# FFT filter and gated FFN in one kernel: batches 1 to 7 transformed inside the FFN of the batch before

## The chip, the cores and the metric

One core of a Trainium2 chip runs the kernel. The metric is device time in microseconds (us). TensorE (PE), VectorE (DVE), ScalarE (ACT) and GpSimd (POOL) compute; SyncE (SP) issues most DMAs; each engine takes its instructions in order.

## What is computed

For eight batches of 3136 positions and 256 channels, a filter is applied in the frequency domain; the result goes through a gated feed-forward network (FFN) with 1024 inner channels.

```python
X = np.fft.rfft(x, axis=1)
Y = X * (filt_r + 1j * filt_i)[None]
x = np.fft.irfft(Y, n=3136, axis=1)

h = np.maximum(x @ w_in, 0.0)
conv_out = sum(conv_w[k] * hp[:, k:k + S, :] for k in range(3))   # hp: h padded by one on both sides
gate = 1.0 / (1.0 + np.exp(-conv_out))
out = (h * gate) @ w_out
```

## The kernel before

**The transform.** 3136 = 112 x 28, so a batch goes through four steps of small f32 matmuls, each in 14 pieces of two column groups. *First* (F, `first`, L317): DFT over 112 rows with the table `s1`, then a copy to SBUF and a store to `a_dram`. *Second* (S, `second`, L324): reads `a_dram` in another order, DFT over 28. *Filter* (`filt`, L334): three DVE multiplications straight from PSUM with the tables `t1` and `t2`, then an addition on POOL. *Third* (T, `third`, L347): inverse over 28 with the table `i1`, a copy and a store to `b_dram`. *Last* (L, `last_stage` and `last_out`, L210 and L219): reads `b_dram`, inverse over 112 with `m2`, and splits the result into a high and a low fp32r part, `y` (ACT writes the high part, DVE subtracts for the low part). Two batches of `y` are held at a time. Going through DRAM turns the data: a batch's S reads need all its F stores, L reads all its T stores.

**The front.** One loop (L366) over 112 pieces of all eight batches, F some 18 pieces ahead of S, filter and T. All tables stay in SBUF; the lower half of the filter tables is copied to the upper partitions by ACT (`copy_filter`). The FFN weights, float64 in DRAM, are converted to fp32 in bits (`to_f32`: seven DVE operations and a POOL addition for each of eight blocks) and split, one step in most iterations. At the end L of batch 0 runs.

**The FFN.** 448 units: a unit is one of 28 stretches of 896 positions (`j`), one of eight groups of 128 inner channels (`f`) and one half of the stretch (`i`). In iteration m each engine has, in the order written out by hand (`manual_schedule`):

- PE: `inner` (six fp32r matmuls into a PSUM bank `ps_h`), an L piece if there is one, `project` of unit m - 6 (4 or 3 tiles of three matmuls into `po`);
- ACT: relu of unit m - 1 and its scaled copy, sigmoid of m - 2, high part of g of m - 3, high part of y of an L piece;
- DVE: two conv steps of unit m - 1, the gate product of m - 2, low part of y, and after the last `f` the copies of `po` (`evacuate`).

The eight PSUM banks are four of `ps_h` (shared by `inner` and L in turn) and four of `po`. L of batch b runs in the FFN of batch b - 1, 14 pieces over its units except those that are 3 to 7 modulo 16:

```python
free = [m for m in range(start, stop) if m % 16 not in AVOID]
```

A copy of `po` comes when m - 6 is the last `f`, so in units 4 and 5 modulo 16. The SP queue is not part of the hand-written order.

Of the kernel before, what the change touches and what calls it, by code (L numbers as in the profile page):

```python
# [9 lines left out]
F32 = mybir.dt.float32  # L10
F32R = mybir.dt.float32r
I32 = mybir.dt.int32
# [7 lines left out]
G = 28  # L20
# [18 lines left out]
def _dft_tables():  # L39
# [68 lines left out]
    i1 = np.concatenate([i1[0], np.zeros((8, G, 112)), i1[1]])  # L108
# [16 lines left out]
def tile_fft_filter_gated_ffn(  # L125
# [5 lines left out]
    nyq: bass.AP,  # L131
# [54 lines left out]
    m2_sb = wc.tile([112, N1], F32, name="m2_sb")  # L186
    cw = wc.tile([128, 3, NF], F32, name="cw")
# [4 lines left out]


    ys, yps = {}, []
    lasts = {}

    def last_load(b, c):
        br = lp.tile([112, 2, D], F32, name="br", bufs=4)
        nc.sync.dma_start(out=br, in_=b_dram[b][c:c + 2].rearrange("n p d -> p n d"))
        lasts[b, c] = br  # L200

    def y_slices(b, sl):
        if sl.start == 0:
            ys[b] = [yps[b % 2].tile([128, KT, S + 2], F32R, name=f"y{h}") for h in range(2)]
            for t in ys[b]:
                nc.gpsimd.memset(t[:, :, 0:1].bitcast(F32), 0.0)
                nc.gpsimd.memset(t[:, :, S + 1:S + 2].bitcast(F32), 0.0)
        return (t[:, :, 1:S + 1].rearrange("p k (a c) -> p k c a", c=N2)[:, :, sl] for t in ys[b])

    def last_stage(b, c, ps):  # L210

        br = lasts[b, c]
        for j in range(2):
            for k in range(KT):
                o = ps[:, (2 * k + j) * N1:(2 * k + j + 1) * N1]
                nc.tensor.matmul(o, lhsT=br[:, j, 128 * k:128 * k + 128], rhs=m2_sb, start=True, stop=True)  # L216
        lasts[b, c] = ps

    def last_out(b, c):  # L219
        yh, yl = y_slices(b, slice(c, c + 2))  # L220
        pv = lasts.pop((b, c))[:, 0:4 * N1].rearrange("p (k c a) -> p k c a", c=2, a=N1)
        hi_act(yh, pv)
        lo_dve(yl, pv, yh)

    forward_pools = ExitStack()
    xp = forward_pools.enter_context(tc.tile_pool(name="xp", bufs=2, side="right"))
    s1_sb = xp.tile([112, N2, 112], F32, name="s1_sb", bufs=1)
    with (
        tc.tile_pool(name="fc", bufs=1) as fc,
        tc.tile_pool(name="fp", bufs=2) as fp,  # L230
# [3 lines left out]
        s2_sb = fc.tile([112, 120], F32, name="s2_sb")  # L234
        s2s_sb = fc.tile([112, 120], F32, name="s2s_sb")
        i1_sb = fc.tile([120, G, 112], F32, name="i1_sb")

        turned = [fc.tile([120, 2, D], F32, name=f"v{k}") for k in range(2)]
        for v in turned:
            nc.gpsimd.memset(v[32:64], 0.0)  # L240
        t1_sb = fc.tile([120, G, D], F32, name="t1_sb")
        t2_sb = fc.tile([120, G, D], F32, name="t2_sb")

        rows = {}

        def load_filter(c):
            sl = slice(4 * c, 4 * c + 4)
            for t, src in ((t1_sb, fr), (t2_sb, fi)):
                nc.sync.dma_start(out=t[0:64, sl], in_=src[:, sl])

        def copy_filter(c):
            sl = slice(4 * c, 4 * c + 4)
            nc.scalar.activation(t1_sb[64:120, sl], t1_sb[0:56, sl], AF.Copy)
            nc.scalar.activation(t2_sb[64:120, sl], t2_sb[0:56, sl], AF.Copy, scale=-1.0)
            if c == 6:
                nc.sync.dma_start(out=t1_sb[92:93, G - 1], in_=nyq)

        raws = {}

        def load_weights(k):  # L260
            raws[k] = raw = cv.tile([128, 2, 512], I32, name="raw")
# [3 lines left out]
        def convert_conv():  # L265
            n = 3 * NF
            raw = cv.tile([128, 2, 512], I32, name="raw")
            nc.sync.dma_start(out=raw[:, 0, 0:2 * n], in_=conv_w)
            yield
            em = cv.tile([128, 2, 512], I32, name="em", bufs=1)  # L270
            yield from to_f32(cw.rearrange("p k f -> p (k f)"), raw[:, 0, 0:2 * n], em[:, 0, 0:n], em[:, 1, 0:n])

        def convert_weights():

            for k in range(8):
# [9 lines left out]
                for part, (wh, wl) in enumerate(parts):  # L285
                    lo_pool(wl, ws[:, part], wh)
                    yield
                if k < 6:
                    load_weights(k + 2)

        NP = 14
        parts = {}
        psums = {}

        def pool(kind):
            return xp if kind in ("x", "sa") else fp

        def load(kind, b, p):
            r = pool(kind).tile([112, 2, D], F32, name=kind, bufs=8 if kind == "x" else 5)
            if kind == "x":  # L300
                v = x[b].rearrange("(p n) d -> p n d", n=N2)
            else:
                v = a_dram[b].rearrange("n (r g) d -> (n r) g d", g=G)
            nc.sync.dma_start(out=r, in_=v[:, 2 * p:2 * p + 2])
            rows[kind, b, p] = r

        def store(kind, b, p, ps):
            st = pool(kind).tile([112, 2, D], F32, name=kind, bufs=4)
            nc.scalar.activation(st, ps, AF.Copy)
            sl = slice(2 * p, 2 * p + 2)  # L310
            if kind == "sa":
                v = a_dram[b][sl].rearrange("n p d -> p n d")
            else:
                v = b_dram[b].rearrange("n (r g) d -> (n r) g d", g=G)[:, sl]
            nc.scalar.dma_start(out=v, in_=st)

        def first(b, p):  # L317
            r = rows.pop(("x", b, p))
            ps = fps.tile([112, 2, D], F32, name="ps")
            for j in range(2):  # L320
                nc.tensor.matmul(ps[:, j], lhsT=s1_sb[:, 2 * p + j], rhs=r[:, j], start=True, stop=True)  # L321
            return ps

        def second(b, p):  # L324
            r = rows.pop(("a", b, p))
            pp = fps.tile([120, 2, D], F32, name="pp", bufs=3)
            if p < NP - 1:
                nc.tensor.matmul(pp, lhsT=s2_sb, rhs=r, start=True, stop=True)  # L328
            else:
                for j, m in ((0, s2_sb), (1, s2s_sb)):  # L330
                    nc.tensor.matmul(pp[:, j], lhsT=m, rhs=r[:, j], start=True, stop=True)
            psums[b, p] = pp

        def filt(b, p):  # L334


            pp, v = psums.pop((b, p)), turned[p % 2]
            sl = slice(2 * p, 2 * p + 2)
            u = fp.tile([120, 2, D], F32, name="u")
            nc.vector.tensor_mul(u, pp, t1_sb[:, sl])  # L340
            nc.vector.tensor_mul(v[64:120], pp[0:56], t2_sb[0:56, sl])  # L341
            nc.vector.tensor_mul(v[0:56], pp[64:120], t2_sb[64:120, sl])  # L342
            z = fp.tile([120, 2, D], F32, name="z", bufs=3)
            nc.gpsimd.tensor_tensor(out=z, in0=u, in1=v, op=ALU.add)  # L344
            parts["z", b, p] = z

        def third(b, p):  # L347
            z = parts.pop(("z", b, p))
            ps = fps.tile([112, 2, D], F32, name="ps")
            for j in range(2):  # L350
                nc.tensor.matmul(ps[:, j], lhsT=i1_sb[:, 2 * p + j], rhs=z[:, j], start=True, stop=True)  # L351
            return ps

        def at(i):
            return divmod(i, NP) if 0 <= i < NP * B else None

        SKEW = NP + 4
        nc.sync.dma_start(out=s1_sb[:, 0:4], in_=s1[:, 0:4])
        load("x", 0, 0)
        load("x", 0, 1)  # L360
        for c in range(1, 4):
            nc.sync.dma_start(out=s1_sb[:, 4 * c:4 * c + 4], in_=s1[:, 4 * c:4 * c + 4])
            load("x", 0, 2 * c)
            load("x", 0, 2 * c + 1)
        csteps, wsteps = convert_conv(), convert_weights()
        done = NP * B + 6  # L366
        NI = max(NP * B + SKEW + 5, done + N2 // 2 + 3)
        with tc.manual_schedule(engines=COMPUTE):
            for i in range(NI):
                f, m = i, i - SKEW  # L370
                if i == done:
                    forward_pools.close()
                    yps.append(ctx.enter_context(tc.tile_pool(name="y_even", bufs=1, side="right", reuse_waits="tile")))
                    lp = ctx.enter_context(tc.tile_pool(name="lp", bufs=2, side="right", reuse_waits="tile"))
                if 1 <= i < 4:
                    nc.sync.dma_start(out=s1_sb[:, 4 * i + 12:4 * i + 16], in_=s1[:, 4 * i + 12:4 * i + 16])
                if (bp := at(f + 7)) and i:
                    load("x", *bp)
                if bp := at(m + 3):
                    load("a", *bp)  # L380
                if i == 6:
# [3 lines left out]
                if 12 <= i < 26 and i % 2 == 0:  # L385
                    sl = slice((i - 12) // 2 * 4, (i - 12) // 2 * 4 + 4)
                    load_filter(i // 2 - 6)
                    nc.sync.dma_start(out=i1_sb[:, sl], in_=i1[:, sl])
                if bp := at(m - 2):
                    filt(*bp)  # L390
                pt = third(*bp) if (bp := at(m - 4)) else None
# [174 lines left out]
```

## Time and profile before

| | |
|---|---|
| median of 3 runs | 1575.55 us (1572.48 to 1576.59) |
| profiled execution, its span | 1573.9 us |
| first FFN matmul (L177) in it | 385.1 us |
| moved by DMA | 166.83 MB |
| mean granted TensorE clock | 0.984 |

The span is the time from the first to the last instruction of one profiled execution; the runs' times are of other executions. In the profile's rows "PE" is a matmul and "PEld" a weight load beside it; "x" gives the count; the last columns of a windows row are granted clock, DMA share and GB/s. A row of the timeline is start, duration, engine, line, and in brackets the idle time before and what ended it.

### The profile page before, as it was taken

What the parts mean: (1) busy time and instruction counts of PE and PEld (TensorE: products, weight loads), DVE (VectorE), ACT (ScalarE), POOL (GpSimd) and SP (SyncE); (2) the same over time, 40 slices, a digit from 0 to 9 for tenths busy, and PEclk for the clock granted to TensorE, in tenths of its full rate; (3) what the DMA queues carried; (4) which work ended last, traced back from release to release, by engine and by line L of the source; (5) the groups of instructions that cost most, each with busy time, mean ns of one, the idle gap of its engine ahead of it and who ended that gap; (6) DMA issues with size and microseconds to landing.
All of it is one profiled execution on the core that took longest, in us unless ns stands there. A gap on an engine that the chain in (4) does not pass through costs nothing.

```text
span 1573.9 us, 26330 instructions
## 1 busy us (share of the span) xinstructions
PE 1510.8 (96%) x9424; PEld 1351.0 (86%) x9424; DVE 1280.7 (81%) x1965; ACT 1192.6 (76%) x2162; POOL 698.0 (44%) x624
## 2 busy tenths in 40 slices
PE   5699999998999999999999999999999999999998
PEld 4366666656999999999999999999999999999998
DVE  0487878897888888888888888888888888888887
ACT  3444444445988888888888888888888888888887
POOL 0255555562444444444444444444444444444444
PEclk8699999999999999999999999999999999999999
DMA  9999999984111011111111111111111111100001
GB/s 292 298 345 349 341 309 338 340 251 142 30 48 48 30 48 48 48 48 48 40 33 36 47 48 49 46 48 47 36 42 48 48 37 41 48 24 25 24 24 48
DMA packets 128278, 166.83 MB, mean 106 GB/s; under 512 B 10682, under 2 KB 87571, under 8 KB 128147
## 3 DMA queue, kind: packets, MB, share of 16 engines
q1 hardware_dynamic: 86931, 113.74, 23.1%
q10 hardware_dynamic: 41216, 51.39, 9.9%
q8 instruction: 75, 1.23, 0.3%
q14 instruction: 56, 0.46, 0.1%
HBM read 88.03 MB, written 77.07 MB: 105 GB/s over the span
## 4 chain that ended last, share of the span: by engine, by line
PE 83%; DMA 9%; DVE 4%; ACT 2%; issue 1%; ACTq 0%; POOL 0%; SPq 0%; DVEq 0%; POOLq 0%
PE ps_h L178 12%; PE ps_h L179 12%; PE ps_h L177 11%; PE po L473 11%; PE po L475 11%; PE po L474 11%; PE ps_h L216 5%; PE ps L321 4%; DMA x<-in_x 3%; PE ps L351 3%; PE pp L328 3%; DMA a<-a_dram 2%; DMA a_dram<-sa 2%; DVE y L149 1%; DVE v L341 1%
## 5 line engine op out<-in xcount | busy, mean ns | idle before, releaser
L152 POOL TENSOR_TENSOR g<-t,g 128x448 fp32r<-128x448 f32 x448 | 517.6, 1156 | 667.6 <-ACT g L146 265.8
L473 PE MATMUL po<-wo,g 128*128 128x256 f32 x1568 | 441.5, 282 | 0.0
L475 PE MATMUL po<-wo,g 128*128 128x256 f32 x1568 | 433.8, 277 | 0.0
L474 PE MATMUL po<-wo,g 128*128 128x256 f32 x1568 | 433.4, 276 | 0.0
L447 DVE SCALAR_TENSOR_TENSOR t<-ps_h,cw,t 128x448 f32<-128x448 f32 x448 | 305.5, 682 | 83.9 <-ACT t L442 73.3
L178 PE MATMUL ps_h<-y,wi 128*128 128x450 f32 x896 | 330.8, 369 | 4.2 <-DVE y L149 4.2
L177 PE MATMUL ps_h<-y,wi 128*128 128x450 f32 x896 | 329.2, 367 | 3.4 <-ACT y L146 2.1
L179 PE MATMUL ps_h<-y,wi 128*128 128x450 f32 x896 | 329.2, 367 | 0.0
L448 DVE SCALAR_TENSOR_TENSOR t<-ps_h,cw,t 128x448 f32<-128x448 f32 x448 | 306.4, 684 | 16.0
L442 ACT ACTIVATE t<-ps_h,cw 128x448 f32<-128x448 f32 x448 | 285.2, 637 | 42.1 <-ACT ps_h L440 0.7
L473 PEld LDWEIGHTS po<-wo,g 128*128 128x128 f32 x1568 | 294.7, 188 | 7.0
L474 PEld LDWEIGHTS po<-wo,g 128*128 128x128 f32 x1568 | 294.3, 188 | 5.7
L475 PEld LDWEIGHTS po<-wo,g 128*128 128x128 f32 x1568 | 294.4, 188 | 0.0
L440 ACT ACTIVATE ps_h<-ps_h 128x450 f32<-128x450 f32 x448 | 251.6, 562 | 32.5 <-PE ps_h L179 27.7
L453 DVE TENSOR_TENSOR t<-ps_h,t 128x448 f32<-128x448 f32 x448 | 275.1, 614 | 0.1
L452 ACT ACTIVATE t<-t 128x448 f32<-128x448 f32 x448 | 255.1, 569 | 12.2 <-DVE t L448 11.0
L146 ACT ACTIVATE g<-t 128x448 fp32r<-128x448 f32 x448 | 254.4, 568 | 0.2 <-DVE t L453 0.2
L344 POOL TENSOR_TENSOR z<-u,v 120x512 f32<-120x512 f32 x112 | 157.2, 1404 | 169.5 <-DVE v L342 144.8
L177 PEld LDWEIGHTS ps_h<-y,wi 128*128 128x128 f32 x896 | 170.4, 190 | 12.0 <-ACT y L146 3.3
L179 PEld LDWEIGHTS ps_h<-y,wi 128*128 128x128 f32 x896 | 168.6, 188 | 13.9
L178 PEld LDWEIGHTS ps_h<-y,wi 128*128 128x128 f32 x896 | 168.6, 188 | 13.5 <-DVE y L149 6.6
L149 DVE TENSOR_TENSOR y<-ps_h,y 128x448 fp32r<-128x448 f32 x98 | 103.1, 1052 | 76.7 <-ACT y L146 76.7
(51 smaller groups left out, 1447.5 us busy)
## 6 DMA issues: line engine op xcount, KB each, us to landing
x<-in_x SPq DMA_DIRECT2D x112, 224.0 KB, 4.6
a_dram<-sa ACTq DMA_DIRECT2D x112, 224.0 KB, 4.5
a<-a_dram SPq DMA_DIRECT2D x112, 224.0 KB, 4.7
b_dram<-sb ACTq DMA_DIRECT2D x112, 224.0 KB, 4.1
br<-b_dram SPq DMA_DIRECT2D x112, 224.0 KB, 2.6
out<-ot SPq DMA_DIRECT2D x27, 896.0 KB, 4.1
raw<-in_w_in SPq DMA_DIRECT2D x8, 256.0 KB, 4.6
raw<-in_w_out SPq DMA_DIRECT2D x8, 256.0 KB, 5.3
```

Source lines behind the costliest of these rows:

```text
L152: nc.gpsimd.tensor_tensor(out=dst, in0=src, in1=hi.bitcast(F32), op=ALU.subtract)
L177: nc.tensor.matmul(ps, lhsT=wh, rhs=rh, start=start, stop=False, **kw)
L178: nc.tensor.matmul(ps, lhsT=wh, rhs=rl, start=False, stop=False, **kw)
L179: nc.tensor.matmul(ps, lhsT=wl, rhs=rh, start=False, stop=stop, **kw)
L442: nc.scalar.activation(t, h[:, 1:SUB + 1], AF.Copy, scale=cw[:, 1, f:f + 1])
L447: nc.vector.scalar_tensor_tensor(out=t, in0=h[:, 0:SUB], scalar=cw[:, 0, f:f + 1], in1=t, op0=ALU.mult, op1=ALU.add)
L448: nc.vector.scalar_tensor_tensor(out=t, in0=h[:, 2:SUB + 2], scalar=cw[:, 2, f:f + 1], in1=t, op0=ALU.mult, op1=ALU.add)
L452: nc.scalar.activation(t, t, AF.Sigmoid)
L453: nc.vector.tensor_mul(t, h[:, 1:SUB + 1], t)
L473: nc.tensor.matmul(o, lhsT=gh[:, sl], rhs=wo[0][:, f], start=first, stop=False, skip_group_check=True)
L474: nc.tensor.matmul(o, lhsT=gh[:, sl], rhs=wo[1][:, f], start=False, stop=False, skip_group_check=True)
L475: nc.tensor.matmul(o, lhsT=gl[:, sl], rhs=wo[0][:, f], start=False, stop=last, skip_group_check=True)
```

## The change

The front keeps the weight conversion, all steps of batch 0, and F of batch 1. F of batches 2 to 7, and S, filter and T of batches 1 to 7, become FFN steps, one step a unit (in nine units of batch 1's stretch two). Steps are laid out in `slots`; their loads are issued three or four units ahead (`loads`, `begin`). The tables are no longer held: each step loads its slice of `s1`, or of both filter halves (now 128 partitions, negation in a DVE operation) and `i1`.

```diff
+    def filt(b, p, pp):
+        t1, t2, v = tables.pop(("t1", b, p)), tables.pop(("t2", b, p)), turned[p % 2]
+        u = tp.tile([120, 2, D], F32, name="u", bufs=1)
+        nc.vector.tensor_mul(u, pp, t1[0:120])
+        nc.vector.tensor_mul(v[64:120], pp[0:56], t2[0:56])
+        nc.vector.scalar_tensor_tensor(out=v[0:56], in0=pp[64:120], scalar=-1.0, in1=t2[64:120], op0=ALU.mult, op1=ALU.mult)
...
+    def store(kind, b, p, ps, eng):
+        st = tp.tile([112, 2, D], F32, name="st")
+        nc.scalar.activation(st, ps, AF.Copy)
...
+        eng.dma_start(out=v, in_=st)
...
+    def second_third(b):
+        seq = [("S", b, 0), ("S", b, 1)]
+        for p in range(2, NP):
+            seq += [("T", b, p - 2), ("S", b, p)]
+        return seq + [("T", b, NP - 2), ("T", b, NP - 1)]
+
+    def first_last(b):
+        seq = [("F", b + 1, p) for p in range(4)]
+        for p in range(4, NP):
+            seq += [("L", b, p - 4), ("F", b + 1, p)]
+        return seq + [("L", b, p) for p in range(NP - 4, NP)]
+
+    slots = {k: [op] for k, op in enumerate(second_third(1))}
+    for p in range(4):
+        slots[2 * NP + p] = [("F", 2, p)]
+    for p in range(NP):
+        slots[32 + p * 15 // (NP - 1)] = [("L", 1, p)]
+    for p in range(4, NP):
+        slots.setdefault(28 + p, []).insert(0, ("F", 2, p))
+    for b in range(2, B):
+        seq = second_third(b)
+        if b < B - 1:
+            seq += first_last(b)
+        for k, op in enumerate(seq):
+            slots[56 * b - 64 + k] = [op]
+    for p in range(NP):
+        slots[56 * B - 88 + p * 23 // (NP - 1)] = [("L", B - 1, p)]
...
+    for m, ops in slots.items():
+        for op in ops:
+            loads.setdefault(m - {"F": 4, "S": 3, "T": 3, "L": 3}[op[0]], []).append(op)
```

The front is three loops: F of batch 0 with the conversion (60 of its 80 steps inside, the rest behind); S, filter and T of batch 0 with ten F pieces of batch 1; L of batch 0 with the last four F pieces. In the FFN `inner` has three PSUM banks (h0 to h2; four once no step is left) and all transform steps the fourth, h3. `gate` loses its sigmoid to a function of its own; every second copy of `po` goes to ACT; the output tile `ot` has one buffer; SP joins the hand-written order and issues the stores. The loop is now:

```diff
+            for s in loads.get(m, ()):
+                begin(s)
+            done, works = works, []
+            ops = slots.get(m, [])
             if a := at(m):
-                inner(*a)
-            if m in pieces:
-                last_stage(*pieces[m], ps_h.tile([128, 512], F32, name="ps_h"))
+                n = 4 if m > end else 3
+                inner(*a, f"h{turn % n}")
+                turn = turn % n + 1
+            if ops:
+                works.append(multiply(ops[0]))
             if a := at(m - PLAG):
                 project(*a)
+            lows = []
             if a := at(m - 1):
                 relu(*a)
-                conv(*a)
+            for w in done[:1]:
+                lows.append(on_act(w))
             if a := at(m - 2):
-                gate(*a)
+                sigmoid(*a)
             if a := at(m - 3):
                 split_g(*a)
-            if m in pieces:
-                last_out(*pieces[m])
+            for w in done[1:]:
+                lows.append(on_act(w))
+            filtered = [w for w in done if w[0][0] == "S"]
+            for (kind, b, p), ps in filtered:
+                filt(b, p, ps)
+            if filtered and (a := at(m - 2)):
+                gate(*a)
+            if a := at(m - 1):
+                conv(*a)
+            for lo in lows:
+                if lo:
+                    lo()
+            if not filtered and (a := at(m - 2)):
+                gate(*a)
+            if ops[1:]:
+                works.append(multiply(ops[1]))
             if a := at(m - PLAG):
                 evacuate(*a)
```

`multiply` runs a step's matmuls into h3. `on_act` runs in the next iteration: the copy and store of an F or T step, or the high part of an L step, whose low part is put in `lows`.

More of the change, by code (lines that the diff above doesn't have):

```diff
@@ new lines, in stage1, with stage2 @@
+    def stage1(b, p, ps):
+        r, t = rows.pop(("x", b, p)), tables.pop(("s1", b, p))
+        for j in range(2):
+            nc.tensor.matmul(ps[:, j], lhsT=t[:, j], rhs=r[:, j], start=True, stop=True)
+    def stage2(b, p, pp):
+        r = rows.pop(("a", b, p))
+        if p < NP - 1:
+            nc.tensor.matmul(pp, lhsT=s2_sb, rhs=r, start=True, stop=True)
+        else:
+            for j, m in ((0, s2_sb), (1, s2s_sb)):
+                nc.tensor.matmul(pp[:, j], lhsT=m, rhs=r[:, j], start=True, stop=True)
@@ new lines, in stage3 @@
+    def stage3(b, p, ps):
+        z, t = parts.pop((b, p)), tables.pop(("i1", b, p))
+        for j in range(2):
+            nc.tensor.matmul(ps[:, j], lhsT=t[0:120, j], rhs=z[:, j], start=True, stop=True)
+    def store(kind, b, p, ps, eng):
+        st = tp.tile([112, 2, D], F32, name="st")
+        nc.scalar.activation(st, ps, AF.Copy)
+        sl = slice(2 * p, 2 * p + 2)
+        if kind == "a":
+            v = a_dram[b][sl].rearrange("n p d -> p n d")
+        else:
+            v = b_dram[b].rearrange("n (r g) d -> (n r) g d", g=G)[:, sl]
+        eng.dma_start(out=v, in_=st)
+        stored[kind, b] = stored.get((kind, b), 0) + 1
@@ L233, in tile_fft_filter_gated_ffn @@
     ):
[L234 to L256, printed above, removed]
         raws = {}
         def load_weights(k):
-            raws[k] = raw = cv.tile([128, 2, 512], I32, name="raw")
+            raws[k] = raw = cv.tile([128, 2, 512], I32, name="raw", bufs=3)
             for part, src in enumerate((w_in, w_out)):
@@ L307, in store @@
[L307 to L367, printed above, removed]
-        with tc.manual_schedule(engines=COMPUTE):
[L369 to L381, printed above, removed]
+                if k < 5:
+                    load_weights(k + 3)
@@ L384, in tile_fft_filter_gated_ffn @@
                     nc.sync.dma_start(out=m2_sb, in_=m2)
[L385 to L391, printed above, removed]
-                pf = first(*bp) if (bp := at(f - 1)) else None
-                if bp := at(m - 1):
-                    second(*bp)
@@ new lines, in tile_fft_filter_gated_ffn @@
+            csteps, wsteps = convert_conv(), convert_weights()
+            for p in range(NP):
+                if p % 2 == 0 and p + 8 < NP:
+                    load_s1_four(p // 2 + 4)
+                if p + 8 < NP:
+                    load_x(0, p + 8, fc, "x", 8)
+                ps = fps.tile([112, 2, D], F32, name="ps")
+                stage1(0, p, ps)
+                store("a", 0, p, ps, nc.scalar)
+                if p == 8:
+                    load_filter_four(0)
+                if p == 10:
+                    load_filter_four(1)
+                if p < 2:
+                    for _ in range(4):
+                        next(csteps, None)
+                else:
+                    for _ in range(5):
+                        next(wsteps, None)
@@ L465, in project @@
         if f == 0 and i == 0:
[L466 removed]
+            pos[j] = [ps_o.tile([128, 512], F32, name=f"po{k}") for k in range(4)], wp.tile([128, NT, D], F32, name="ot", bufs=1)
         po, ot = pos[j]
@@ L494, in tile_fft_filter_gated_ffn, with multiply @@
     NH = 16 * (B * S // CH)
-    pieces = {}
-    for b in range(1, B):
-        start = ((NSUB * (b - 1) - 1) // 2 + 1) * 16 + (4 if b == 1 else 0)
-        stop = NSUB * b // 2 * 16 + NSUB * b % 2
-        free = [m for m in range(start, stop) if m % 16 not in AVOID]
-        for c in range(N2 // 2):
-            pieces[free[c * (len(free) - 1) // (N2 // 2 - 1)]] = (b, 2 * c)
+    def multiply(s):
+        kind, b, p = s
+        ps = ps_h.tile([128, 512], F32, name="h3")
+        wide = ps.rearrange("p (n d) -> p n d", d=D)
+        if kind == "F":
+            stage1(b, p, wide[0:112])
+            return s, wide[0:112]
+        if kind == "S":
+            stage2(b, p, wide[0:120])
+            return s, wide[0:120]
+        if kind == "T":
+            stage3(b, p, wide[0:112])
+            return s, wide[0:112]
+        last_stage(b, 2 * p, ps)
+        return s, ps
```

240 lines of the change are left out of this document (169 added, 71 removed).

## The prediction

> **What bounds the kernel now.** I read the page first (busy times, the 40 slices), then the windows on both sides of the first FFN matmul, at 385.1 us.
>
> ```profile
> PE 1510.8 (96%) x9424; PEld 1351.0 (86%) x9424; DVE 1280.7 (81%) x1965; ACT 1192.6 (76%) x2162; POOL 698.0 (44%) x624
> PE   5699999998999999999999999999999999999998
> DMA  9999999984111011111111111111111111100001
> ...
> 0.00:385.10 385.10, 331.45 (x1248) 220.09 (x1248) 275.30 (x413) 168.47 (x270) 179.43 (x148) 0.95 0.96 307
> 385.10:1573.90 1188.80, 1179.35 (x8176) 1130.95 (x8176) 1005.45 (x1553) 1024.14 (x1892) 518.60 (x476) 1.00 0.13 41
> 60.00:340.00 280.00, 258.41 (x955) 169.37 (x954) 227.87 (x343) 123.75 (x210) 153.76 (x117) 0.97 1.00 328
> ```
>
> Two stages with two limits. In the front (385.1 us) the DMA engines are 96% busy, from 60 to 340 us 100% at 328 GB/s: it is bound by transfers. The FFN (1188.8 us) has PE busy 1179 us and DMA at 0.13: it is bound by PE alone. Moving transforms into the FFN frees DMA-bound time and puts PE work on the engine that has none to spare. So the prices of a transform step on PE come next: timeline rows of PE, in the front where steps follow each other, and in the FFN around a last-stage piece.
>
> ```profile
> 286.31 1.03 PE L321 MATMUL ps<-x,s_sb 112*112 112x256 f32 x4
> 287.18 1.02 PE L328 MATMUL pp<-a,s_sb 112*120 112x512 f32 x2
> 288.04 1.03 PE L351 MATMUL ps<-z,i_sb 120*112 120x256 f32 x4
> 288.90 1.03 PE L321 MATMUL ps<-x,s_sb 112*112 112x256 f32 x4
> ...
> 802.86 1.04 PE L216 MATMUL ps_h<-m_sb,br 112*128 112x112 f32 x8
> 803.66 0.37 PE L473 MATMUL po<-wo,g 128*128 128x256 f32 x1
> 803.87 0.28 PE L474 MATMUL po<-wo,g 128*128 128x256 f32 x1
> 803.99 0.28 PE L475 MATMUL po<-wo,g 128*128 128x256 f32 x1
> ```
>
> Start to start, a first (F), second (S) or third (T) step is 0.86 us. A last-stage piece (L) is 0.80, and the projection matmul behind it takes 0.21 instead of 0.11: 0.10 for leaving f32.
>
> The other scale is a unit without transform, near the end of the run:
>
> ```profile
> 1485.32 0.37 PE L177 MATMUL ps_h<-y,wi 128*128 128x450 f32 x1
> 1486.55 0.28 PE L473 MATMUL po<-wo,g 128*128 128x256 f32 x1
> 1487.91 0.37 PE L177 MATMUL ps_h<-y,wi 128*128 128x450 f32 x1
> 1489.14 0.28 PE L473 MATMUL po<-wo,g 128*128 128x256 f32 x1
> 1490.16 0.37 PE L177 MATMUL ps_h<-y,wi 128*128 128x450 f32 x1
> ...
> 1484.50 0.53 ACT L440 ACTIVATE ps_h<-ps_h 128x450 f32<-128x450 f32 x1 [0.40 <-PE ps_h L179]
> 1485.12 0.64 ACT L442 ACTIVATE t<-ps_h,cw 128x448 f32<-128x448 f32 x1
> 1485.66 0.57 ACT L452 ACTIVATE t<-t 128x448 f32<-128x448 f32 x1
> ...
> 1485.79 0.68 DVE L447 SCALAR_TENSOR_TENSOR t<-ps_h,cw,t 128x448 f32<-128x448 f32 x1 [0.65 <-ACT t L442]
> 1486.51 0.68 DVE L448 SCALAR_TENSOR_TENSOR t<-ps_h,cw,t 128x448 f32<-128x448 f32 x1
> 1487.12 0.61 DVE L453 TENSOR_TENSOR t<-ps_h,t 128x448 f32<-128x448 f32 x1
> ```
>
> The input product takes 1.24 us, a projection 1.36 (four tiles, even units) or 1.02 (three, odd units). Counted from a unit's first matmul: product readable at 1.40, relu 1.44, scale 2.06 (+0.62), next on ACT 2.59 (+0.53), first conv step on DVE 2.73 (+0.67), second 3.45, next on DVE 4.06. These offsets decide what the change costs.
>
> **Term 1: the front, gain.** It keeps the weight conversion, all of batch 0 and F of batch 1. Counted from the diff's sizes it moves some 36 MB, at 328 GB/s 110 us at least. But three phases follow one another. The rows of the group listing and of the DMA issues:
>
> ```profile
> 0.00:385.10 385.10, 31.71 (x63) 10.37 (x9) 0.95 0.96 307
> L174 POOL TENSOR_TENSOR ws<-ws,em 128x512 f32<-128x512 f32 x8 | 10.1, 1267 | 0.0
> L146 ACT ACTIVATE y<-ps 128x448 fp32r<-128x448 f32 x14 | 14.1, 1006 | 5.4 <-ACT sb L309 5.4
> L309 ACT ACTIVATE sb<-ps 112x512 f32<-112x512 f32 x112 | 66.7, 596 | 96.2 <-PE ps L351 36.9 <-DMA a<-a_dram 24.0 <-PE ps L321 12.5
> a_dram<-sa ACTq DMA_DIRECT2D x112, 224.0 KB, 4.5
> a<-a_dram SPq DMA_DIRECT2D x112, 224.0 KB, 4.7
> b_dram<-sb ACTq DMA_DIRECT2D x112, 224.0 KB, 4.1
> br<-b_dram SPq DMA_DIRECT2D x112, 224.0 KB, 2.6
> ```
>
> (The first row is the windows view of tile em, the scratch of the conversion: busy time of DVE, then POOL.) (a) All eight weight blocks are now converted ahead of the first filter step in DVE's order. A block is 3.8 us of DVE (31.7 less 1.3 for conv_w, by 8), then 1.27 on POOL, and em has one buffer: 5.3 us with the hops, 43 us in all, from about 8 us (estimate: first weights behind 1.3 MB): to 51 us. F of batch 0, its stores (4.5) and first reads (4.7) end just inside that. (b) S, filter and T of batch 0 and ten F steps move 15 MB: 46 us. (c) The last stage waits for the last store (4.1) and its read (2.6), then 14 pieces at 1.01 on ACT and four stores of F: 25 us. First FFN matmul at 122 us: **-263**. Bounds: 110 by bytes, 140 if each phase takes 6 us more.
>
> **Term 2: PE work in the FFN, loss.** F of batches 2 to 7 (84 steps), S and T of 1 to 7 (98 each): 280 steps. 0.86 each is 241 us. No row shows such a step between fp32r matmuls; the nearest, L, says 0.10 more for leaving, so 0 to 28 us; I take 28: **+269**. L of batches 1 to 7 was there before and stays.
>
> **Term 3: waits in the FFN, loss.** All transforms share one PSUM bank, h3. The next unit's step, second in PE's order, waits until the bank is read, and the unit's projection and all later matmuls queue behind it. The reader of F and T is a store copy on ACT right after relu: 2.59 to 3.2 us. For S it is three filter steps on DVE, whose spacing the front shows:
>
> ```profile
> 249.72 0.69 DVE L340 TENSOR_TENSOR u<-pp,t_sb 120x512 f32<-120x512 f32 x1
> 250.44 0.68 DVE L341 TENSOR_TENSOR v<-pp,t_sb 56x512 f32<-56x512 f32 x1
> 251.15 0.69 DVE L342 TENSOR_TENSOR v<-pp,t_sb 56x512 f32<-56x512 f32 x1
> ```
>
> S ends at 2.3, the filter at 4.45. PE wants the bank after step, projection and next product: 1.24 + 0.96 + 1.02 + 1.24 = 4.46 in an odd unit, 4.8 in an even one. S sits in odd units, so it just fits, at no slack. For L the reader ends with the subtraction on DVE behind both conv steps:
>
> ```profile
> L149 DVE TENSOR_TENSOR y<-ps_h,y 128x448 fp32r<-128x448 f32 x98 | 103.1, 1052 | 76.7 <-ACT y L146 76.7
> L488 DVE COPY ot<-po 128x512 f32<-128x512 f32 x83 | 54.2, 679 | 3.2 <-PE po L475 3.2
> ```
>
> 4.06 + 1.05 = 5.11, wanted at 4.73: 0.4 us. Seventy pieces of batches 2 to 6 give 29 us; batch 1, with F and L in nine units, 1.1 each and a little: 14 us.
>
> The larger price is the evacuation. In two of 16 units (4 and 5 modulo 16) DVE and now ACT copy po at the end of the unit's orders, so both wait for that unit's projection before they take the next relu, store or filter. Before, the copies waited for PE 3.2 us in 110 (row L488): units were 2.4 us, DVE came late anyway, and the pieces avoided units 3 to 7. Now the projection starts 0.96 later and no unit is left out. Even unit with T: projection readable at 3.72, copy on ACT, relu at 4.29 instead of 1.44, store done 6.04, bank wanted at 4.79: 1.3 us. Odd unit with S: its filter stands behind a copy that waits for po, 1.4 us. Even unit with L: relu 4.24, conv from 5.53, subtraction done 7.9, wanted 4.73: 3.2 us; the F behind it 1.1, the next L 0.6 more. Two L's in a row: 3.2 and 3.0. By the slots: ten S/T pairs at 2.7, five L/F at 4.5, three L/L at 5.4, two F/F at 2.4 and 6 us for the doubled units: 77 us. Five more for the first units, which have no projection to hide behind. **+125**. Bounds: nothing (the row L488 as it is now) to 160 (S late as well, 0.3 us each for 98).
>
> **At nothing.** Filter and table loads: an S/T pair moves 1072 KB in some 6.7 us, 164 GB/s, half of what the front sustained; a load is issued three units (10 us) ahead against 4.7 us to landing. SP now issues the stores too, and its loads stand behind a store that waits for ACT; that is one unit of the three. If the lead is lost, S waits, up to 2 us a pair, 200 us in all. DVE's load is 2 x 1.85 + 2.15 = 5.9 us a pair and a share of copies, below 6.7. Three instead of four product banks: the gate ends about 4.8 us after the product starts and the bank returns at 6.7 or later. FFN's last 64 units and the tail are as before.
>
> **Sum.** 1573.9 - 263 + 269 + 125 = 1705 in the profiled execution, 1.65 below the median of the runs: 1706.
>
> A page of the Trainium skill speaks against the change once more. The row first: at the FFN's start, after a sparse stretch, matmuls follow at 0.38 us instead of 0.205.
>
> ```profile
> 387.06 0.58 PE L177 MATMUL ps_h<-y,wi 128*128 128x450 f32 x1
> 387.44 0.58 PE L178 MATMUL ps_h<-y,wi 128*128 128x450 f32 x1
> ```
>
> The Trainium skill, "TensorE: Matmul & The Clock Gate", section "Why this matters for your kernels", says that gaps of more than about 3 us between matmul bursts bring the half clock back. By it the 3.2 us stalls would each be followed by a slow stretch of some 3.4 us, about 14 us in all, and the sum would be 1720. The row agrees with the half clock; that a single gap of that length suffices, no run here shows, and I leave it out.
>
> **Rivals.**
> (1) *Only the bank waits, not the evacuation*: ACT and DVE come to the copies late enough, as they do now. For it: 3.2 us in 110 copies. Against it: the 0.96 us in front of the projection. 1706 - 77 = 1629.
> (2) *Faster: the steps slip in without a wait.* Mechanism: the h3 bank is always read in time, leaving f32 costs nothing, and the front runs at its bytes, 110 us. It decides where waits and leaving together stay below 275 - 241 = 34 us. Price: 1575.6 - 275 + 241 = 1542. For it: PE's front steps follow at 0.86 without gaps. Against it: L already misses by 0.4 us in every unit. With the front at 122 and the 28 us paid but no wait it is 1582, about no change.
> (3) *Data or DVE late*: S has no slack, so any lateness of DVE or of SP's loads is paid 98 times; 0.6 us each is 60 us: 1765.
>
> **How the numbers follow.** Forecast (1640 to 1750) 0.55, rival 1 (1595 to 1640) 0.18, rival 2 0.15 (1542 to 1582), rival 3 0.12. The range of 8 in 10 takes the forecast, rival 1 and half of rival 3: 1600 to 1755. A measurement here tells about 0.3%, 5 us, from no change. Faster comes from rival 2 alone: 0.11; within 0.3% 0.04; the rest is slower: 0.85.
>
> **What would show it.** First L177-type matmul at 110 to 140 us; PE idle in the FFN some 120 us, ended by DVE's subtraction and by ACT's store copy, in pairs of units 16 apart; DVE and ACT idle before the po copies, waiting for PE, 60 us or more instead of 3.2; DMA around 0.4 in the FFN, with no PE wait for loads. A stall-free FFN (PE at 99%) would refute term 3; PE waiting on DMA would show rival 3; steps at 0.86 without the 0.10 would lower term 2.

## The result and the profile after

The changed kernel takes 1757.49 us (median of 4, 1756.22 to 1762.02) against 1576.07 us for the kernel before on the same chip: a ratio of 1.1154, with an interval of 1.1128 to 1.1179. The forecast was 1706 us and its range 1600 to 1755. The direction came out as forecast; the time is 51 us above the forecast and 2.5 us above the upper end.

The page of the changed kernel, with the rows that answer to those of before:

```profile
PE 1577.0 (90%) x9424; PEld 1364.2 (78%) x9424; DVE 1251.5 (71%) x1911; ACT 1208.0 (69%) x2216; POOL 679.8 (39%) x624
PE   4468997899998999899989999989998899999998
PEclk7588999999999999999999999999999999999999
DMA  8687544555444545345443554445544445220001
```

The FFN now begins in the fourth slice, and PE is no longer busy throughout it. The windows view, cut where DVE's queue reaches the first filter step (the step itself starts 0.6 us later), at the last T matmul of batch 0 and at the first FFN product (columns as before: span, then PE, PEld, DVE, ACT and POOL busy, clock, DMA share, GB/s):

```profile
0.00:59.90 59.90, 24.86 (x60) 14.66 (x61) 34.33 (x63) 18.82 (x34) 22.86 (x29) 0.68 0.87 258
59.90:121.60 61.70, 43.09 (x114) 24.25 (x113) 29.56 (x43) 21.72 (x31) 20.46 (x21) 0.76 0.69 206
121.60:152.20 30.60, 20.69 (x139) 18.66 (x137) 11.31 (x13) 17.42 (x23) 0.00 (x0) 0.83 0.92 267
...
152.20:1755.00 1602.80, 1488.31 (x9114) 1306.59 (x9114) 1176.31 (x1794) 1150.09 (x2128) 636.47 (x574) 0.99 0.42 127
```

The front ends at 152.2 us, 233 us earlier than before, 30 later than forecast. Its second phase is the weak one: 206 GB/s at a DMA share of 0.69 means that transfers don't bound it. The FFN grew by 414 us, from 1188.8 to 1602.8. The waits view of the FFN (microseconds in all, times, longest):

```profile
ACT ot L566 <- PE po L555: 126.3, 50, 4.5
DVE ot L568 <- PE po L555: 44.9, 36, 2.8
...
PEld h L257 <- issue: 51.3, 91, 1.6
...
PEld h L232 <- DVE y L148: 39.2, 53, 1.3
```

ACT and DVE wait 171 us for `po` before they copy it, where DVE waited 3.2 us before. PE's T steps (L257) wait after S, which the profile puts under "issue", and its F steps (L232) wait for the low part of L (L148). No row has PE waiting for a DMA in the FFN.

To size the terms I took the start of each unit's first product (L176) and subtracted the product's and projection's times. Units without a step and away from the copies show no excess at all (0.00 us in 55 units), so the rest is exact to some hundredths a unit.

| term | forecast | measured |
|---|---|---|
| 1: first FFN product | 122 | 152.2 |
| 2: 280 steps in the FFN | 269 (0.96 each) | about 250 (0.89 to 0.92 each) |
| 3: waits in the FFN | 125 | some 170 |
| of these: copies of `po` | 77 | 87 |
| one bank, L | 29 | 32 |
| one bank, S | 0 | 23 |
| nine doubled units and around | 14 | 21 |
| first units | 5 | 8 |

Since the FFN before held a few microseconds of waits too, the difference of the two FFNs leaves 164 for term 3 (1602.8 - 1188.8 - 250). The misses are then +30, -19 and +39: together 50, and 1705 + 50 is the span of 1755.

One stall, whole. The timeline, PE's rows first, then ACT's, then DVE's:

```profile
965.03 1.11 PE L289 MATMUL h<-m_sb,br 112*128 112x112 f32 x8 [3.00 <-issue]
...
966.92 0.28 PE L555 MATMUL po<-wo,g 128*128 128x256 f32 x1
967.03 0.37 PE L176 MATMUL h<-y,wi 128*128 128x450 f32 x1
...
971.21 2.02 PE L289 MATMUL h<-m_sb,br 112*128 112x112 f32 x8 [2.79 <-issue]
972.90 0.56 PE L553 MATMUL po<-wo,g 128*128 128x256 f32 x1
973.26 0.41 PE L554 MATMUL po<-wo,g 128*128 128x256 f32 x1
973.48 0.42 PE L555 MATMUL po<-wo,g 128*128 128x256 f32 x1
...
967.23 0.39 ACT L566 ACTIVATE ot<-po 128x256 f32<-128x256 f32 x1 [2.92 <-PE po L555]
967.51 0.54 ACT L517 ACTIVATE h<-h 128x450 f32<-128x450 f32 x1
968.15 0.63 ACT L519 ACTIVATE t<-h,cw 128x448 f32<-128x448 f32 x1
968.68 0.97 ACT L145 ACTIVATE y<-h 128x448 fp32r<-128x448 f32 x1
...
968.81 0.68 DVE L524 SCALAR_TENSOR_TENSOR t<-h,cw,t 128x448 f32<-128x448 f32 x1 [1.23 <-ACT t L519]
969.53 0.68 DVE L525 SCALAR_TENSOR_TENSOR t<-h,cw,t 128x448 f32<-128x448 f32 x1
970.13 0.97 DVE L148 TENSOR_TENSOR y<-h,y 128x448 fp32r<-128x448 f32 x1
```

ACT stood 2.92 us before its copy, until the projection ended at 967; only then came relu, scale and high part, on DVE conv and the low part, which ends at 971.10. PE's next L piece starts at 971.21. This is the forecast chain, link by link. And something follows that the forecast had left out: the projection behind this stall runs at 0.21 us a matmul instead of 0.11, and the L piece takes 1.69 instead of 0.88 (from 971.21 to 972.90, and from 965.03 to 965.91). That is half speed. It isn't the rule after every stall: the one at 965.03, of 3.00 us, is followed by full speed. Of 14 stalls with more than 2.2 us from one matmul start to the next, six have such a stretch behind them, 1.5 to 2.8 us each, 12 us in all.

### The profile page after: what moved, and what is told of

The parts are those of the page before. It is cut to its first block, busy times and chain, and to the rows that moved or that the text cites. A ratio compares the mean times of both kernels' runs of the same rounds, so it can differ in the third digit from the quotient of the medians.

```text
span 1755.0 us, 26959 instructions
## 1 busy us (share of the span) xinstructions
PE 1577.0 (90%) x9424; PEld 1364.2 (78%) x9424; DVE 1251.5 (71%) x1911; ACT 1208.0 (69%) x2216; POOL 679.8 (39%) x624
## 4 chain that ended last, share of the span: by engine, by line
PE 72%; DVE 9%; ACT 8%; DMA 5%; issue 4%; POOL 0%; SPq 0%; ACTq 0%; DVEq 0%
PE po L553 9%; PE po L555 9%; PE po L554 9%; PE h L176 8%; PE h L177 8%; PE h L178 8%; PE h L257 6%; PE h L232 5%; PE h L237 5%; DVE y L148 4%; ACT t L519 3%; PE h L289 3%; ACT h L517 2%; DVE t L524 2%; DVE t L525 2%
## 5 line engine op out<-in xcount | busy, mean ns | idle before, releaser
L553 PE MATMUL po<-wo,g 128*128 128x256 f32 x1568 | 518.8, 331 | 0.0
L524 DVE SCALAR_TENSOR_TENSOR t<-h,cw,t 128x448 f32<-128x448 f32 x448 | 304.9, 681 | 250.1 <-ACT t L519 249.6
L554 PE MATMUL po<-wo,g 128*128 128x256 f32 x1568 | 440.7, 281 | 0.0
L555 PE MATMUL po<-wo,g 128*128 128x256 f32 x1568 | 440.4, 281 | 0.0
L517 ACT ACTIVATE h<-h 128x450 f32<-128x450 f32 x448 | 238.4, 532 | 236.2 <-PE h L178 233.8
L176 PE MATMUL h<-y,wi 128*128 128x450 f32 x896 | 334.0, 373 | 6.7 <-DVE t L533 5.1
L177 PE MATMUL h<-y,wi 128*128 128x450 f32 x896 | 331.4, 370 | 1.3 <-DVE y L148 1.3
L178 PE MATMUL h<-y,wi 128*128 128x450 f32 x896 | 329.3, 368 | 0.0
L553 PEld LDWEIGHTS po<-wo,g 128*128 128x128 f32 x1568 | 299.0, 191 | 30.3 <-issue 21.5
L554 PEld LDWEIGHTS po<-wo,g 128*128 128x128 f32 x1568 | 298.7, 190 | 27.0 <-issue 20.9
L525 DVE SCALAR_TENSOR_TENSOR t<-h,cw,t 128x448 f32<-128x448 f32 x448 | 306.5, 684 | 16.0
L519 ACT ACTIVATE t<-h,cw 128x448 f32<-128x448 f32 x448 | 284.3, 635 | 42.3 <-ACT h L517 1.5
L555 PEld LDWEIGHTS po<-wo,g 128*128 128x128 f32 x1568 | 297.7, 190 | 0.0
L533 DVE TENSOR_TENSOR t<-h,t 128x448 f32<-128x448 f32 x448 | 277.0, 618 | 6.9 <-ACT t L529 3.8
L176 PEld LDWEIGHTS h<-y,wi 128*128 128x128 f32 x896 | 171.2, 191 | 17.1 <-DVE t L533 7.2
L178 PEld LDWEIGHTS h<-y,wi 128*128 128x128 f32 x896 | 169.8, 190 | 14.2
L177 PEld LDWEIGHTS h<-y,wi 128*128 128x128 f32 x896 | 170.6, 190 | 9.0 <-issue 2.3
L251 POOL TENSOR_TENSOR z<-u,v 120x512 f32<-120x512 f32 x112 | 143.5, 1281 | 82.3 <-DVE v L249 66.0
L289 PEld LDWEIGHTS h<-m_sb,br 112*128 112x128 f32 x784 | 103.7, 197 | 40.5 <-issue 19.5
```

Source lines behind the costliest of these rows:

```text
L176: nc.tensor.matmul(ps, lhsT=wh, rhs=rh, start=start, stop=False, **kw)
L177: nc.tensor.matmul(ps, lhsT=wh, rhs=rl, start=False, stop=False, **kw)
L178: nc.tensor.matmul(ps, lhsT=wl, rhs=rh, start=False, stop=stop, **kw)
L517: nc.scalar.activation(h, h, AF.Relu)
L519: nc.scalar.activation(t, h[:, 1:SUB + 1], AF.Copy, scale=cw[:, 1, f:f + 1])
L524: nc.vector.scalar_tensor_tensor(out=t, in0=h[:, 0:SUB], scalar=cw[:, 0, f:f + 1], in1=t, op0=ALU.mult, op1=ALU.add)
```

## The experiments

My theory after the result: the copies of `po` and the single bank make the waits, and the front is late because of its buffers and queues, not its bytes. Rivals: the step itself is dear (whatever stands around it), moving copies to ACT costs nothing, DVE is just too slow. Runs with an interval are given with it; the others are single executions beside a kernel before of 1576.74 to 1578.71 us. How far single executions scatter, the traces show: in the changed kernel and the five runs that edit only the front, the FFN takes 1599.9 to 1607.7 us; in the changed kernel and the six that edit only the FFN, the first FFN product comes at 150.3 to 154.0 us.

### Project first

The transform step goes behind the projection in PE's order, so that the projection doesn't come 0.9 us later for it.

```diff
-            if ops:
-                works.append(multiply(ops[0]))
             if a := at(m - PLAG):
                 project(*a)
+            if ops:
+                works.append(multiply(ops[0]))
```

> Edit: in each FFN unit PE runs the projection before the transform step instead of after it. Theory A (the FFN's 169 us of waits come from the shared bank h3, whose reader in the next iteration ends after PE wants the bank, and from copies of po that hold ACT and DVE until the projection ends): the projection ends 0.9 us earlier in its unit and the bank is wanted 1.0 to 1.4 us later, while relu starts as before; waits fall to 60 us or less, time 1640 to 1660, step prices (0.9 us) unchanged. Rival R (ACT and DVE are simply full, PE waits for their work whatever the order): within 10 us of 1757.

1640.89 us, ratio 1.0391 (1.0368 to 1.0415): 117 us less, as expected. Waits in the FFN fall from 170 to 56 us: the copies from 87 to 18, the F behind an L from 24 to 5.5. Two reasons act together: the projection is readable one step earlier for the copies, and the bank h3 is wanted later. The next run parts them. ACT's waits for `po` from 160 to 1600 us, first of the changed kernel, then of this one:

```profile
ACT ot L566 <- PE po L555: 117.6, 44, 4.5
```

```profile
ACT ot L566 <- PE po L555: 39.5, 27, 1.9
```

They are a third of what they were, and the longest is 1.9 us instead of 4.5. None of the 14 long stalls is left, and none of the slow stretches.

### Copies one unit later

`evacuate` runs one iteration later; PE's order stays as in the changed kernel.

```diff
-        for m in range(NH + PLAG):
+        for m in range(NH + PLAG + 1):
...
-            if a := at(m - PLAG):
+            if a := at(m - PLAG - 1):
                 evacuate(*a)
```

> Edit: the copies of po are ordered one iteration later, when their projection has long ended. Theory A: only the waits in the units after units 4 and 5 modulo 16 (87 us) shrink, to some 15; the 0.3 us after S and the 0.5 us after L in the other units stay: 1675 to 1700. Rival R: the copies cost the same work, so within 10 us of 1757.

1667.01 us, ratio 1.056 (1.0535 to 1.0585): 90 us less, more than expected. The waits at the copies go from 87 to 8 us, those around the doubled units from 21 to 13; the F behind an L stays at 21 (24), the T behind S at 23. This shows the price of the evacuation by itself, and that the waits on the single bank are another matter. The long stalls are gone, and with them the 12 us of half speed, which the expectation had not counted.

### All copies on DVE

```diff
-                if k % 2:
+                if end and k % 2:
                     nc.scalar
```

> Edit: all copies of po on DVE again, that part of the change undone. Theory A: relu no longer stands behind a copy, so a T or F step in an evacuation unit makes no wait (now 1.3), L waits about 2.1 instead of 3.5, S a little more: 20 to 35 us less, 1722 to 1738. If moving copies to ACT had paid by relieving DVE: 5 to 20 us more than 1757.

1708.14 us, 49 us less, beyond the expected gain. The copies' share of the waits is 48 instead of 87 us.

```profile
DVE ot L568 <- PE po L555: 38.5, 34, 2.2
```

This is DVE's wait for `po` from 160 to 1600 us with all copies on it. ACT has none there, so relu and stores come on time. No stall above 2.2 us is left, but 10 us of the FFN still run at half clock (27 in the changed kernel), at a loss of up to 5 us; so some 7 of the 12 us are among the 49. About half of what the evacuation costs stems from its being put on a second in-order engine: 49 of 90 us, or 39 of 79 by the copies' share alone.

### Project first and copies later together

> Edit: projection ahead of the step (as e1_project_first) and the copies of po one iteration later (as e2_evac_late). Theory A: what is left of evacuation waits after the reordering alone (17 us of 56) goes, the rest stays: 1615 to 1630. If the two remove the same waits: within 5 us of 1641.

1632.99 us, ratio 1.0361 (1.0344 to 1.0378): 3 us short of the expected bounds. Copies 3.5 us, 46 us of waits in all. The two edits overlap, as they should if both remove the same wait: together 124 us, singly 117 and 90.

### T three pieces behind S, so that S falls in even units

The order of S and T is shifted by one unit; an even unit's projection is 0.34 us longer, which gives the filter that much time.

```diff
-        seq = [("S", b, 0), ("S", b, 1)]
-        for p in range(2, NP):
-            seq += [("T", b, p - 2), ("S", b, p)]
-        return seq + [("T", b, NP - 2), ("T", b, NP - 1)]
+        seq = [("S", b, 0), ("S", b, 1), ("S", b, 2)]
+        for p in range(3, NP):
+            seq += [("T", b, p - 3), ("S", b, p)]
+        return seq + [("T", b, p) for p in range(NP - 3, NP)]
```

> Edit: each T step one place later, so that S falls in even units, whose projection has four tiles. Theory A: the 0.3 us wait after S (23 us in all) is missing slack of PE against the three filter steps; 0.34 us more projection behind S removes it: the T steps' units have no wait, time 1730 to 1742. Rival: the 0.3 us is the price of going from one f32 step kind to the other: no change, 1757.

1738.35 us, 19 us less. The waits of T behind S fall from 22.7 to 4.1 us. The timeline of the changed kernel, PE and then DVE:

```profile
806.88 1.02 PE L237 MATMUL h<-xa,s_sb 112*120 112x512 f32 x2
...
809.84 0.36 PE L178 MATMUL h<-y,wi 128*128 128x450 f32 x1
810.21 1.09 PE L257 MATMUL h<-z,i1t 120*112 120x256 f32 x4
...
812.52 0.37 PE L176 MATMUL h<-y,wi 128*128 128x450 f32 x1
...
808.00 0.69 DVE L247 TENSOR_TENSOR u<-h,t 120x512 f32<-120x512 f32 x1 [0.94 <-POOL g L151]
808.72 0.68 DVE L248 TENSOR_TENSOR v<-h,t 56x512 f32<-56x512 f32 x1
809.42 0.69 DVE L249 SCALAR_TENSOR_TENSOR v<-h,t 56x512 f32<-56x512 f32 x1
```

The filter ends at 810.11, 4.46 us after the unit began at 805.65, as forecast (4.45). But the bank was wanted at 810.04: 4.39 instead of 4.46, since the step took 0.90 instead of 0.96. With 0.10 from the filter's end to T's start the slack of nothing became a wait of 0.2 to 0.3 us, and T stands behind S in over 80 units.

### Low part ahead of the conv steps

DVE takes L's subtraction before the two conv steps instead of behind them.

```diff
-            if a := at(m - 1):
-                conv(*a)
             for lo in lows:
                 if lo:
                     lo()
+            if a := at(m - 1):
+                conv(*a)
```

> Edit: DVE subtracts for the low part of y ahead of the two conv steps. Theory A: an L step's bank is free 1.05 us after its high part, at 4.7 us of its unit instead of 5.1, as PE wants it: the 0.5 us wait after L (24 us in all) and some 1.3 us of each L in an evacuation unit go: 1717 to 1732. Rival: conv, gate and the three product banks come late in turn and PE waits for the gate instead: 1750 or more.

1746.84 us: 11 us less in one execution, between the theory and the rival, and not far above the scatter. The F behind an L waits 8 instead of 24 us, as the theory had it. But the units behind an L without a step of their own, which had no wait, now lose 8 us: the conv steps come later and hold the product banks. DVE also waits 194 us (98 times) for ACT's high part where it waited 24. Half of the gain comes back as another wait. Half clock covers 41 us of this FFN and 27 of the changed kernel's, which hides up to 6 us more.

### Two buffers for u

In the front's second phase filter steps of DVE follow 3.58 us apart, as the one buffer `u` waits for POOL.

```diff
-        u = tp.tile([120, 2, D], F32, name="u", bufs=1)
+        u = tp.tile([120, 2, D], F32, name="u", bufs=2)
```

> Edit: two buffers for u, the product that DVE hands to POOL, as before the change. Theory: in the front's second phase the filter chain repeats every 3.58 us because the next product waits for POOL's addition (1.27); with two buffers the chain is 2.15 and the phase ends on transfers: first FFN matmul 5 to 12 us earlier than 152, FFN unchanged. Rival: the phase is held by the SP queue (reads of a behind filter loads that wait for a buffer) and moves under 3 us.

1758.42 us, first FFN product at 153.0 (152.2): no change, so the rival is right here. SP's waits from 60 to 130 us show what holds the phase, first of the changed kernel, then of this one:

```profile
SPq L393 <- PE ps L257: 14.5, 4, 5.0
```

```profile
SPq L393 <- PE ps L257: 19.9, 4, 7.9
```

L393 loads `i1` into one of three buffers and waits for a T step to free it. Behind it in SP's queue stand the reads of `a_dram` for coming S steps. A faster filter only makes SP wait longer.

### Four buffers for i1, alone and with two for u

```diff
-            it = fc.tile([128, 4, 112], F32, name="i1c", bufs=3)
+            it = fc.tile([128, 4, 112], F32, name="i1c", bufs=4)
```

> Edit: in the front four buffers for a block of i1, and u with one. Theory: the SP queue's wait for i1 was the longer of two chains, the filter chain through u (3.58 us a piece, 14 pieces) the next: first FFN matmul at 143 to 149 us, between 152 (none) and 140.8 (both). If i1 alone gives the whole gain, u plays no part: 140 to 142.

> Edit: in the front four buffers for a block of i1 (three now) and two for u. Theory: with u alone nothing moved because SP, in order, holds the reads of a behind the load of i1, which waits 15 to 20 us in all for a T step to free its buffer; with both, the second phase is bound by transfers: first FFN matmul at 138 to 145 us instead of 152. Rival: the next wait of SP (filter tables, three buffers) takes its place, under 4 us.

Alone: first FFN product at 146.5; with two `u`: 140.8. Both are within what was expected, and so the two chains lie one behind the other: the queue first, then `u`. The times are 1755.97 and 1742.64 us; the first shows little of its 6 us, since its FFN was 5 us longer in this execution. Its trace has 51 us of the FFN at half clock, in place of 27 in the changed kernel's: up to 11 us lost more, which covers the 5. The phases, from the same three points as above:

| kernel | to the first filter | to the last T | to the FFN | first product at |
|---|---|---|---|---|
| forecast | 51 | 46 | 25 | 122 |
| changed kernel | 59.9 | 61.7 | 30.6 | 152.2 |
| four i1 | 58.9 | 55.3 | 32.3 | 146.5 |
| four i1, two u | 59.2 | 47.4 | 34.2 | 140.8 |

With both buffers the second phase is as long as the forecast had it by bytes (46), in part by luck: 11.9 MB at 250 GB/s, where the forecast had 15 MB at 328. The last phase gives back 4 of the 14 us.

### Conversion spread over the front

Both buffers, the reads of `a_dram` ahead of the table loads, and two instead of five conversion steps with each F piece, so that the filter starts before the conversion ends.

```diff
-                    for _ in range(5):
+                    for _ in range(2):
                         next(wsteps, None)
...
-            for _ in range(25):
-                next(wsteps, None)
```

> Edit: front only: u and i1 as in e10, reads of a ordered ahead of filter loads, and two instead of five conversion steps for each F piece, the rest beside S, filter and T of batch 0. Theory: F of batch 0 no longer waits on ACT behind the conversion (store of its last piece at 46 us now, about 30 then), and the first filter step no longer stands behind all eight blocks (60 us now, about 40 then): first FFN matmul at 120 to 132 us, near the prediction's term, time 1725 to 1737. Rival: the front's end is set by its transfers at the rate it has now (240 GB/s): 145 or later.

1751.48 us, first FFN product at 149.8, a miss: worse than with the buffers alone. DVE's queue does reach the first filter step early, at 36.6 us. But DVE then stands idle until S gives it its input, since the reads of `a_dram` come late, and the step starts at 50.8 us instead of 60.5. After that it has the rest of the conversion between the filter steps. The windows view of 50 to 100 us (PE, PEld, DVE, ACT, POOL):

```profile
50.00:100.00 50.00, 34.41 (x73) 15.81 (x72) 47.64 (x58) 15.60 (x25) 28.50 (x23) 0.72 0.74 211
```

DVE is full, 47.6 of 50 us, and its integer steps have grown, in the same kernel's timeline:

```profile
50.75 0.69 DVE L247 TENSOR_TENSOR u<-pp,t1c 120x512 f32<-120x512 f32 x1 [18.55 <-PE pp L237]
...
52.91 0.43 DVE L159 TENSOR_SCALAR em<-raw 128x512 int32<-128x512 int32 x1
53.26 1.49 DVE L161 TENSOR_SCALAR em<-raw 128x512 int32<-128x512 int32 x1
54.78 1.10 DVE L163 TENSOR_TENSOR em<-em 128x512 int32<-128x512 int32 x1
55.92 0.83 DVE L165 TENSOR_SCALAR em<-raw 128x512 int32<-128x512 int32 x1
```

### Two buffers for em

```diff
-        em = cv.tile([128, 2, 512], I32, name="em", bufs=1)
+        em = cv.tile([128, 2, 512], I32, name="em", bufs=2)
```

> Edit: two buffers for em, the scratch of the conversion. Theory: a block of weights costs 6.1 us in the front's first phase because the next block waits for POOL's addition; F of batch 0 and its stores stand behind it on ACT, so the phase ends 5 to 9 us earlier and the first FFN matmul comes at 143 to 147 us. Rival: the blocks wait for their 512 KB from DRAM (DVE waits for raw, up to 4.8 us) and for DVE's slower integer steps beside POOL: under 3 us.

1756.0 us, first FFN product at 151.0, the first filter step in DVE's queue at 58.2 (59.9): a gain of 1.2 to 1.7 us at most, within the scatter, so the rival's case. The one buffer, which the forecast named as what spaces the blocks, isn't what makes the first phase late.

### The sum

Project first, copies one unit later, two `u`, four `i1`, two `em`.

> Edit: the two FFN edits of e6_both with the front's buffers (u two, i1 four, em two). Theory: front and FFN add up, the front 11 to 13 us shorter as with e10 and e11, the FFN as in e6_both: 1618 to 1624. What then stands against the kernel before is the price of 280 steps on PE (250 us) and some 45 us of waits, against a front about 245 us shorter: slower by 2.5 to 3.2%. If the FFN's waits change when the first units start earlier: off by more than 5 us.

1618.57 us, ratio 1.0262 (1.0244 to 1.0279): 139 us better than the changed kernel, still 2.6% slower than the kernel before. The windows view of its FFN:

```profile
137.80:1614.80 1477.00, 1454.18 (x9114) 1310.93 (x9114) 1187.55 (x1794) 1147.55 (x2128) 639.29 (x574) 1.00 0.46 138
```

PE is busy 98% of it. Against the kernel before: the front gives 247 us (385.1 - 137.8), the steps take some 250, and about 38 of waits are left (1477.0 - 1188.8 - 250). That is the whole of the 41 us between the spans (1614.8 and 1573.9). Without any wait it would be about a draw. No version that I ran beats the kernel before.

## Why the prediction was right, and where it failed

**Where the 51 us lie.** Three steps failed. Term 1 made the front's phases too short (+30). Term 3 put two things at nothing: the lateness of S, which measured 23 us, and the half clock, 12 us, of its +39. Term 2 was too dear (-19) and hid part of this.

**What bounds the kernel.** Right. The front was bound by transfers and the FFN by PE, so work moved from one to the other is traded, about one for one: 233 us gained, 250 paid before any wait. That leaves no gain, and the waits make the loss.

**Term 1, the front, failed**, by 30 us of the 50. All three phases were put too short. Phase (a), "5.3 us with the hops, 43 us in all", left out that the raw weights would not always be there. DVE's blocks of conversion, and POOL's additions beside them, in the timeline:

```profile
21.76 0.43 DVE L159 TENSOR_SCALAR em<-raw 128x512 int32<-128x512 int32 x1 [3.17 <-DMA raw<-in_w_out]
31.24 0.43 DVE L159 TENSOR_SCALAR em<-raw 128x512 int32<-128x512 int32 x1 [4.80 <-DMA raw<-in_w_out]
...
39.10 0.69 DVE L163 TENSOR_TENSOR em<-em 128x512 int32<-128x512 int32 x1
...
43.61 0.43 DVE L159 TENSOR_SCALAR em<-raw 128x512 int32<-128x512 int32 x1 [1.37 <-POOL ws L173]
44.41 1.09 DVE L163 TENSOR_TENSOR em<-em 128x512 int32<-128x512 int32 x1
...
49.72 0.43 DVE L159 TENSOR_SCALAR em<-raw 128x512 int32<-128x512 int32 x1 [1.37 <-POOL ws L173]
...
37.73 0.72 POOL L151 TENSOR_TENSOR wo<-ws,wo 128x256 fp32r<-128x256 f32 x1
...
44.91 1.17 POOL L151 TENSOR_TENSOR wo<-ws,wo 128x256 fp32r<-128x256 f32 x1
```

The middle blocks wait up to 4.80 us for their transfer, and the later ones are 6.1 us apart instead of 5.3, as two of their steps lengthen beside a POOL addition (L163: 1.09 instead of 0.69). Phase (b), 46 us for 15 MB, took bytes for the limit of a phase whose queue and buffers had not been looked at; the two buffer runs show that these are the 14 us. Phase (c) was 6 us short: L's first piece starts 11.6 us after the last T, as the store of that T stands behind two others on ACT, and L's first two pieces share ACT with copies of F.

**Term 2 was too large by 19 us**: only the size was off. A step costs 0.89 to 0.92 us between fp32r matmuls. Of the 0.10 for leaving f32, taken from L's row, 0.03 to 0.06 are there; I had taken the upper end.

**Term 3 was right in its mechanism and too small.** Pairs of units 16 apart lose what the chain of ACT and DVE gives: behind an odd unit with S 1.5 us (forecast 1.4), behind an even one with T 1.3 (1.3), F behind L 3.7 (3.2), L behind F 1.2 (1.1), two L's in a row 3.3 and 4.4 (3.2 and 3.0). The two that were sized low were so by the clock alone: where no half clock followed, F behind L cost 3.2 us (three of five) and the second L 3.0 (one of three). The step of this term that failed is "it just fits, at no slack": a sum of modelled offsets that ends at nothing was costed at nothing, and it was 23 us. The price was in the text, in the bound "S late as well, 0.3 us each for 98".

**The clock.** The Trainium skill, "TensorE: Matmul & The Clock Gate", section "Why this matters for your kernels", says that gaps of more than about 3 us bring the half clock back. The changed kernel agrees in six of 14 stalls, down to one of 2.62 us from start to start, and disagrees in eight, of up to 3.37; the last section has what tells them apart. The forecast's estimate by that page was 14 us; 12 were lost. Leaving it out was wrong.

**At nothing.** Right for the loads: DMA at 0.42 in the FFN, no wait of PE for one. DVE's own load was hidden too, at 73% busy in the FFN.

**The rivals.** The first, no price for the evacuation, is refuted: late copies alone gave 90 us. The second, faster, needed waits and leaving f32 together below 34 us; the best version has some 47 (38, and 9 for leaving) and a front 28 us longer than that rival's. The third named the right sufferer, S, at less than half the lateness that it had (0.2 to 0.3 us for 0.6). Its cause, data or a late DVE, isn't what the traces show: no wait of PE for a load, and a filter that ends at 4.46 us as forecast. PE came early, and shifting S by one unit cured it.

## What to carry to other kernels

When work moves from a stage bound by transfers to one bound by an engine, compare first what the front gives and what that engine takes: here 233 and 250 us, and no schedule could win much. Then follow one unit through every in-order engine: a small step ahead of a matmul that others wait for costs little itself, while the engines that wait for it hold up everything behind them: copies one unit later were worth 90 us here, and the order of two PE operations 117. A sum that ends at zero slack should be costed as a small wait times its count, and a phase that is short enough to be bound by buffers should not be costed by bytes.

## What the hardware showed unexpectedly

DVE's integer steps on SBUF lengthen while POOL adds: a TENSOR_TENSOR from 0.69 to 1.09 or 1.10 us, a TENSOR_SCALAR from 0.43 to 0.83 and up to 1.49, and POOL's own additions from 0.72 to 1.17. The filter steps, which read PSUM, kept 0.69 beside the same POOL work. The Trainium skill, "SBUF — State Buffer", section "SBUF: two separate sides", says that DVE and GpSimd share one pair of ports as an exclusive lock, taken by a DVE instruction with two SBUF inputs or in a mode with two ports. That an engine waits for the other's turn fits these lengths, and so do the filter steps with only one input in SBUF; no run here tested it by itself.

A stall of PE of some 3 us was followed by half speed in some cases and not in others of the same length. The granted clock of the same trace tells them apart. In the FFN the half clock comes in stretches of 3.41 us, or two of them in a row, and their starts (902.14, 970.40 and 1390.24 us, for example) lie whole multiples of 3.41 us apart, as if on a fixed grid. The windows view, cut on this grid around the stalls that end at 965.03 and 971.21:

```profile
960.16:963.57 3.41, 1.86 (x12) 1.42 (x10) 1.59 (x3) 2.64 (x5) 0.00 (x0) 1.00 0.44 135
963.57:966.98 3.41, 1.95 (x17) 1.99 (x18) 1.96 (x4) 0.74 (x2) 1.15 (x1) 1.00 0.78 253
966.98:970.40 3.42, 1.44 (x8) 1.00 (x7) 2.15 (x4) 3.08 (x7) 0.00 (x0) 1.00 0.53 179
970.40:973.81 3.41, 2.60 (x12) 2.63 (x13) 2.61 (x4) 1.70 (x4) 1.14 (x1) 0.50 0.99 277
```

The first stall, 3.00 us long, falls across two intervals (1.55 and 1.46 us of PE idle), and the clock stays full. Of the second, 2.79 us long, 1.98 us lie in one interval, and the next has half clock. In the changed kernel's FFN each half clock that follows full clock has an interval with at least 1.96 us idle before it, and no interval at full clock that has 1.78 us or less is followed by one. Over all runs the border lies between 1.76 and 1.90 us, about half an interval. So whether a stall of this length costs more than itself depends on where it falls; no run here moved a stall on purpose.
